# First layer's cosine: one read of PSUM, the argument in turns, and 2 pi applied to the stored sums

## The chip, the cores and the metric

The kernel runs on one core of one Trainium2 chip. The metric is the device time of one execution in microseconds (us); lower is better. Within the core, TensorE (PE in the profile) multiplies, VectorE (DVE), ScalarE (ACT) and GpSimd (POOL) work elementwise, and SyncE (SP) issues the transfers. They run at the same time and meet at semaphores. Each takes its own instructions in a fixed order.

## The reference

An attention with packed keys, then two layers of the same build, each a product, an elementwise function and a second product. The change lies in the elementwise function of the first layer, `h * cos(h)`.

```python
def _attn_ref(q, k, v, p):                     # (8, 8, 576, 64); p: (8, 8, 32, 64)
    p_packed = sm_attn(p, k, v)                # softmax attention of 32 queries per head
    return sm_attn(q, p_packed, p_packed)

def _moe_ref(x, w_in, w_out):                  # first layer: x (4608, 512), w_in (512, 2048)
    h = x @ w_in
    g = h * np.cos(h)
    return (g @ w_out).astype(np.float32)

def _moe2_ref(x, w_in, w_out):                 # second layer
    h = x @ w_in
    sp = np.where(h > 20.0, h, np.log1p(np.exp(np.minimum(h, 20.0))))
    return ((h * np.tanh(sp)) @ w_out).astype(np.float32)

x = attn_out.transpose(0, 2, 1, 3).reshape(B * S, H * D)
x = _moe_ref(x=x, **moe_kwargs)
return _moe2_ref(x=x, **moe2_kwargs)
```

All tensors are fp32 (weights come in as 64-bit numbers and are converted on the chip).

## The kernel before, in words

The program has two stages. Stage one holds the attention and the first layer, stage two the second layer. This text calls 40 to 845 us of the profiled execution stage one's main part: it is where the 256 units described next run.

The 4608 tokens are cut into 16 tiles of 288, and the 2048 columns of the hidden layer into 16 slices of 128. A *unit* is one slice of one tile, so `h` comes in 256 blocks of 128x288. For a unit, TensorE first computes `h` with six matmuls (`l1`): every fp32 operand is kept as a high part rounded to fp32r and a low rest, and `mm3` adds three products (lines L145, L146, L147; two such triples for the two halves of the inner dimension). The result lies in one buffer of a PSUM ring of four, named `ps`. The same ring serves the attention's matmuls, in the background.

Then comes the chain of elementwise work of the unit:

- `chain_first`: ACT reads `ps`, scales by 1/(2 pi), adds 0.25 and rounds to an integer `ki` (L802). DVE reads `ki` and `ps` and forms `r = ps - 2 pi * ki` (L804). DVE clamps `r` to the range that the sine takes (L805).
- `chain_cos`: ACT computes `sin(r + pi/2)` in place (L811). DVE multiplies it by `ps` (L812). This is the last read of `ps`, and frees the ring's buffer.
- `chain_split`: ACT rounds the product to the high part `gh[:, 0]` (L819; `G_ACT = (0, 1)` with `G_MOD = 2` puts every unit there), and POOL computes the low part `gh[:, 1]` (L822), which frees the buffer of `r` (four of them).

Three units behind, `l2` multiplies `gh` by the second weight `wo` with twelve matmuls into four PSUM accumulators `acc` (again L145 to L147). After 16 units, `evac` copies the four accumulators to SBUF, two on ACT (L843) and two on DVE (L845), and stores them to DRAM (`x2d`), where stage two picks them up.

Between the units' instructions stands background work for later tiles: loads, transposes, softmax and projections of the attention, conversions of weights (L436, L437, L441, L581 to L583), and splits of weights for stage two. The source says after how many units each piece is given out. The order on each engine, though, is made by the framework's scheduler, which runs the program against its own model of durations, with priorities written in the source (`HP_L1`, `HP_CHAIN`, and others). A changed duration or dependency can therefore move instructions anywhere in stage one.

DVE operations are told apart below by where their tensor inputs lie: L804 and L812 have one input in SBUF and one in PSUM; L441 has two in SBUF; L805 has one, in SBUF.

Of the kernel before, what the change touches and what calls it, by code (L numbers as in the profile page):

```python
# [8 lines left out]
F32 = mybir.dt.float32  # L9
F32R = mybir.dt.float32r  # L10
I32 = mybir.dt.int32
AF = mybir.ActivationFunctionType
ALU = mybir.AluOpType
# [5 lines left out]
TT = 288  # L19
# [3 lines left out]
NBT = NTOK // BT  # L23
LAG_A = 3
G_MOD = 2
G_ACT = (0, 1)
C_MOD = 2
C_POOL = ()
W_POS = ((57, 1.1), (55, 1.2), (52, 1.2))
K_LD = 3  # L30
Q_LD = 2
# [51 lines left out]
TWO_PI = 2.0 * math.pi  # L83
# [4 lines left out]
def build(tc, q, k, v, p, w1i, w1o, w2i, w2o, out):  # L88
    nc = tc.nc
    ctx = ExitStack()  # L90
    with ctx:
        wpool = ctx.enter_context(tc.tile_pool(name="wpool", bufs=1))
# [5 lines left out]
        def nm(s):  # L98
            cnt[0] += 1
            return f"{s}_{cnt[0]}"  # L100
# [17 lines left out]

        ident = wpool.tile([128, 128], F32, name="ident")
        make_identity(nc, ident)  # L120
        halfpi = wpool.tile([128, 1], F32, name="halfpi")
        nc.vector.memset(halfpi, math.pi / 2)
        quarter = wpool.tile([128, 1], F32, name="quarter")
        nc.vector.memset(quarter, 0.25)
        wpool.tile([128, 8], F32, name="gap_w")
# [6 lines left out]
        ap = apool_cm.__enter__()  # L132
# [575 lines left out]
        for j in range(16):  # L708
            ms[j], load, cs = w_load(j // 4, j % 4, True)
            n = W0_STEP[j]  # L710
# [7 lines left out]
        for ft in range(16):  # L718
            load, cs = wo1_unit(ft)
            n = ft + WO_OFF  # L720
# [9 lines left out]
        for j in range(16):  # L730
            ms[j], load, _ = w_load(j // 4, j % 4)
            n = W01[0] + int(W01[1] * j)
# [20 lines left out]
        for pair in range(3):  # L753
# [9 lines left out]
            for j in range(16):  # L763
                ms[j], load, _ = w_load(j // 4, j % 4)
                n = n0 + W_POS[pair][0] + int(W_POS[pair][1] * (j // 2 * 2 + 1))
# [5 lines left out]
        for t in range(1, NT):  # L771
            n = Q_N[t - 1]
# [25 lines left out]

        def chain_first(n):
            st = hst[n]  # L800
            ki = ap.tile([128, TT], I32, tag="ki", bufs=2, name=nm("ki"))
            nc.scalar.activation(ki, st["h"], AF.Identity, bias=quarter, scale=1.0 / TWO_PI)  # L802
            r = ap.tile([128, TT], F32, tag="r", bufs=4, name=nm("r"))
            nc.vector.scalar_tensor_tensor(r, ki, -TWO_PI, st["h"], ALU.mult, ALU.add)  # L804
            (nc.gpsimd if n % C_MOD in C_POOL else nc.vector).tensor_scalar(r, r, 1.570796, -4.712388, ALU.min, ALU.max)  # L805
            st["r"] = r

        def chain_cos(n):
            st = hst[n]
            g = st["r"]  # L810
            nc.scalar.activation(g, g, AF.Sin, bias=halfpi, scale=1.0)  # L811
            nc.vector.tensor_tensor(g, g, st["h"], ALU.mult)  # L812
            st["g"] = g

        def chain_split(n):
            st = hst[n]
            gh = ap.tile([128, 2, TT], F32R, tag="gh", bufs=GH_BUFS, name=nm("gh"))
            if n % G_MOD in G_ACT:
                nc.scalar.copy(gh[:, 0], st["g"])  # L819
# [17 lines left out]
        def evac(t):  # L837
            for dc in range(4):
                o = ap.tile([128, TT], F32, tag="xo", bufs=3, name=nm("xo"))
                x = acc[t][dc][:, :TT].rearrange("p (a s) -> p s a", s=32)  # L840
                y = o.rearrange("p (s a) -> p s a", s=32)
                if dc % 2 == 0:
                    nc.scalar.copy(y, x)  # L843
                else:
                    nc.vector.tensor_copy(y, x)  # L845
                nc.sync.dma_start(x2d[t][:, dc, :], o)

        X = {}
# [62 lines left out]
        for n in range(NA + LAG_A):  # L911
            if STOP and n >= STOP:
                apool_cm.__exit__(None, None, None)
                return
            if n < NA:
                with tc.high_priority(offset=HP_L1):
                    l1(n)
            run_bg(bg_pe, n)
            m = n - LAG_A
            if m >= 0:  # L920
                l2(m)
            with tc.high_priority(offset=HP_CHAIN):
                if 1 <= n <= NA:
                    chain_cos(n - 1)
                if n < NA:
                    chain_first(n)
                if 1 <= n <= NA:
                    chain_split(n - 1)
            run_ew(n)
            if m >= 0 and m % NF == NF - 1:  # L930
                evac(m // NF)
# [268 lines left out]
```

## Time and profile before

| | |
|---|---|
| median of 3 runs | 1555.14 us (1553.41 to 1558.32) |
| the profiled execution's own time | 1555.48 us |
| its span, first to last instruction | 1552.9 us |
| PE, PEld busy | 1475.9 us (95%), 1278.3 us (82%) |
| DVE, ACT, POOL busy | 1117.8 (72%), 883.9 (57%), 639.2 us (41%) |
| mean granted TensorE clock | 0.989 of full speed |

PE is the matmul side of TensorE, PEld its loading of weights, which overlaps the matmuls. A busy PE is not a PE at its peak: in full flow the matmuls of stage one start 0.13 us apart and each is shown as about 0.3 us long, so their spans overlap. What matters is the idle time before an instruction and the instruction that ended it (the *releaser*). A wait of PE means that matmuls had run out; a wait of PEld means that the next weights could not be loaded, which comes a little earlier.

### The profile page before, as it was taken

What the parts mean: (1) busy time and instruction counts of PE and PEld (TensorE: products, weight loads), DVE (VectorE), ACT (ScalarE), POOL (GpSimd) and SP (SyncE); (2) the same over time, 40 slices, a digit from 0 to 9 for tenths busy, and PEclk for the clock granted to TensorE, in tenths of its full rate; (3) what the DMA queues carried; (4) which work ended last, traced back from release to release, by engine and by line L of the source; (5) the groups of instructions that cost most, each with busy time, mean ns of one, the idle gap of its engine ahead of it and who ended that gap; (6) DMA issues with size and microseconds to landing.
All of it is one profiled execution on the core that took longest, in us unless ns stands there. A gap on an engine that the chain in (4) does not pass through costs nothing.

```text
span 1552.9 us, 28652 instructions
## 1 busy us (share of the span) xinstructions
PE 1475.9 (95%) x9728; PEld 1278.3 (82%) x9728; DVE 1117.8 (72%) x2082; ACT 883.9 (57%) x1838; POOL 639.2 (41%) x634
## 2 busy tenths in 40 slices
PE   3789999999999999999999999999999999999998
PEld 1567778788987898788999887888889898888997
DVE  4896666777776877678675878678668857766756
ACT  3675767666667677667665455344443534454443
POOL 0462333245643544627754666223522622352102
PEclk9899999999999999999999999999999999999999
DMA  9889676436648457533313767668868877877887
GB/s 293 283 214 226 170 184 161 123 101 176 186 122 225 139 152 195 163 107 104 104 49 98 259 217 241 193 196 242 266 212 235 298 223 219 244 205 221 241 257 202
DMA packets 247377, 300.75 MB, mean 194 GB/s; under 512 B 104384, under 2 KB 129472, under 8 KB 247232
## 3 DMA queue, kind: packets, MB, share of 16 engines
q1 hardware_dynamic: 246432, 298.73, 66.1%
q8 instruction: 77, 1.26, 0.3%
q14 instruction: 68, 0.56, 0.1%
q10 hardware_dynamic: 800, 0.20, 0.1%
HBM read 242.22 MB, written 56.62 MB: 192 GB/s over the span
## 4 chain that ended last, share of the span: by engine, by line
PE 50%; DVE 6%; ACT 3%; issue 2%; DMA 2%; POOL 1%; SPq 0%; DVEq 0%; ACTq 0%; POOLq 0%
PE acc L146 9%; PE acc L147 9%; PE acc L145 9%; PE ps L145 8%; PE ps L147 8%; PE ps L146 8%; DVE r L805 1%; ACT r L811 1%; DVE r L812 1%; DVE r L804 1%; DMA raw<-in_moe_w_in_dram 1%; DVE wab L897 1%; ACT wab L896 1%; PE ps L491 0%; DMA tst<-wt 0%
## 5 line engine op out<-in xcount | busy, mean ns | idle before, releaser
L822 POOL TENSOR_TENSOR gh<-r,gh 128x288 fp32r<-128x288 f32 x256 | 214.9, 847 | 334.3 <-ACT gh L819 231.7
L146 PE MATMUL acc<-gh,wo 128*128 128x288 f32 x1024 | 301.5, 301 | 2.2 <-POOL gh L822 1.7
L147 PE MATMUL acc<-gh,wo 128*128 128x288 f32 x1024 | 298.2, 298 | 0.0
L955 POOL TENSOR_TENSOR gh<-t,gh 128x512 fp32r<-128x512 f32 (+1 forms) x108 | 144.2, 1340 | 351.5 <-ACT gh L954 290.7
L145 PE MATMUL acc<-gh,wo 128*128 128x288 f32 x1024 | 273.7, 304 | 2.1 <-ACT gh L819 1.9
L145 PEld LDWEIGHTS acc<-gh,wo 128*128 128x128 f32 x1024 | 181.2, 190 | 34.6 <-issue 11.9
L146 PE MATMUL acc<-gh,T 128*128 128x512 f32 (+1 forms) x560 | 207.0, 371 | 2.2 <-DVE gh L955 1.7
L145 PE MATMUL ps<-wab,ws 128*128 128x512 f32 (+1 forms) x560 | 206.0, 369 | 1.8 <-ACT gh L954 0.8
L146 PEld LDWEIGHTS acc<-gh,wo 128*128 128x128 f32 x1024 | 194.1, 190 | 15.9 <-issue 9.5
L146 PE MATMUL ps<-wab,ws 128*128 128x512 f32 (+1 forms) x560 | 206.4, 369 | 0.0
L147 PE MATMUL ps<-wab,ws 128*128 128x512 f32 (+1 forms) x560 | 205.4, 369 | 0.0
L147 PE MATMUL acc<-gh,T 128*128 128x512 f32 (+1 forms) x560 | 205.1, 369 | 0.0
L147 PEld LDWEIGHTS acc<-gh,wo 128*128 128x128 f32 x1024 | 194.2, 190 | 5.8 <-issue 5.6
L955 DVE TENSOR_TENSOR gh<-wo,gh 128x512 fp32r<-128x512 f32 (+1 forms) x160 | 128.7, 810 | 81.7 <-ACT gh L954 81.3
L811 ACT ACTIVATE r<-r,halfpi 128x288 f32<-128x288 f32 x256 | 136.3, 535 | 83.9 <-DVE r L805 81.6
L145 PE MATMUL acc<-gh,T 128*128 128x512 f32 (+1 forms) x560 | 181.9, 369 | 0.6 <-DMA T<-tst 0.5
L145 PE MATMUL ps<-aT,wab 128*128 128x288 f32 x512 | 159.7, 312 | 22.7 <-DVE r L812 16.5
L812 DVE TENSOR_TENSOR r<-r,ps 128x288 f32<-128x288 f32 x256 | 114.5, 449 | 73.3 <-ACT r L811 72.5
L802 ACT ACTIVATE ki<-ps,quarter 128x288 int32<-128x288 f32 x256 | 125.1, 496 | 59.7 <-PE ps L147 49.6
L804 DVE SCALAR_TENSOR_TENSOR r<-ki,ps 128x288 f32<-128x288 int32 x256 | 113.8, 447 | 55.8 <-ACT ki L802 39.5
L146 PE MATMUL ps<-aT,wab 128*128 128x288 f32 x512 | 152.2, 297 | 0.0
L147 PE MATMUL ps<-aT,wab 128*128 128x288 f32 x512 | 151.5, 296 | 0.0
(169 smaller groups left out, 2956.1 us busy)
## 6 DMA issues: line engine op xcount, KB each, us to landing
T<-tst SPq DMA_DIRECT2D x280, 256.0 KB, 3.1
ws<-wst SPq DMA_DIRECT2D x224, 256.0 KB, 3.0
ld<-ws SPq DMA_DIRECT2D x80, 256.0 KB, 3.5
kr<-in_k_dram SPq DMA_DIRECT2D x64, 272.0 KB, 5.6
kr<-in_q_dram SPq DMA_DIRECT2D x60, 272.0 KB, 6.0
tst<-wt SPq DMA_DIRECT2D x56, 256.0 KB, 2.6
wst<-ws SPq DMA_DIRECT2D x56, 256.0 KB, 2.5
x2d<-xo SPq DMA_DIRECT2D x64, 144.0 KB, 1.8
```

What stands on the lines that cost most here:

```text
L145: nc.tensor.matmul(ps, l0, r0, start=first, stop=False, skip_group_check=more)
L146: nc.tensor.matmul(ps, l0, r1, start=False, stop=False, skip_group_check=more)
L147: nc.tensor.matmul(ps, l1, r0, start=False, stop=last, skip_group_check=more)
L802: nc.scalar.activation(ki, st["h"], AF.Identity, bias=quarter, scale=1.0 / TWO_PI)
L804: nc.vector.scalar_tensor_tensor(r, ki, -TWO_PI, st["h"], ALU.mult, ALU.add)
L805: (nc.gpsimd if n % C_MOD in C_POOL else nc.vector).tensor_scalar(r, r, 1.570796, -4.712388, ALU.min, ALU.max)
L811: nc.scalar.activation(g, g, AF.Sin, bias=halfpi, scale=1.0)
L812: nc.vector.tensor_tensor(g, g, st["h"], ALU.mult)
L822: nc.gpsimd.tensor_tensor(gh[:, 1], st["g"], gh[:, 0], ALU.subtract)
L896: nc.scalar.copy(x[:, a, 0, :n], src)
L897: (nc.gpsimd if k % 2 == 0 else nc.vector).tensor_tensor(x[:, a, 1, :n], src, x[:, a, 0, :n], ALU.subtract)
L955: eng.tensor_tensor(hl[:, 1, :n], src, hl[:, 0, :n], ALU.subtract)
```

## The change

`f = h / (2 pi)` is written once from PSUM to SBUF by ACT, with no added constant (first instruction). A second ACT instruction reads `f` from SBUF, adds 0.25 and rounds to the integer `ki`, which lies in the bytes of `u`. One DVE operation then forms `u = f + 0.25 - ki`, between -0.5 and 0.5, so that no clamp is needed. The sine takes `2 pi * u`, without an added tensor, and DVE multiplies it by `f` instead of by `ps`. Since `f` is `h / (2 pi)`, the sums of the second product come out divided by 2 pi, and `evac` multiplies them by 2 pi where it copied them before. `G_ACT = (0,)` gives the rounding of the high part to ACT in every even unit and to DVE in every odd one.

```diff
-G_ACT = (0, 1)
-C_MOD = 2
-C_POOL = ()
+G_ACT = (0,)
...
         def chain_first(n):
             st = hst[n]
-            ki = ap.tile([128, TT], I32, tag="ki", bufs=2, name=nm("ki"))
-            nc.scalar.activation(ki, st["h"], AF.Identity, bias=quarter, scale=1.0 / TWO_PI)
-            r = ap.tile([128, TT], F32, tag="r", bufs=4, name=nm("r"))
-            nc.vector.scalar_tensor_tensor(r, ki, -TWO_PI, st["h"], ALU.mult, ALU.add)
-            (nc.gpsimd if n % C_MOD in C_POOL else nc.vector).tensor_scalar(r, r, 1.570796, -4.712388, ALU.min, ALU.max)
-            st["r"] = r
+            f = st["f"] = ap.tile([128, TT], F32, tag="f", bufs=4, name=nm("f"))
+            nc.scalar.activation(f, st["h"], AF.Identity, scale=1.0 / TWO_PI)
+            u = st["u"] = ap.tile([128, TT], F32, tag="u", bufs=2, name=nm("u"))
+            ki = u.bitcast(I32)
+            nc.scalar.activation(ki, f, AF.Identity, bias=quarter)
+            nc.vector.scalar_tensor_tensor(u, f, 0.25, ki, ALU.add, ALU.subtract)

         def chain_cos(n):
             st = hst[n]
-            g = st["r"]
-            nc.scalar.activation(g, g, AF.Sin, bias=halfpi, scale=1.0)
-            nc.vector.tensor_tensor(g, g, st["h"], ALU.mult)
-            st["g"] = g
+            f, u = st["f"], st["u"]
+            nc.scalar.activation(u, u, AF.Sin, scale=6.283185)
+            nc.vector.tensor_tensor(f, f, u, ALU.mult)
+            st["g"] = f
...
                 if dc % 2 == 0:
-                    nc.scalar.copy(y, x)
+                    nc.scalar.mul(y, x, TWO_PI)
                 else:
-                    nc.vector.tensor_copy(y, x)
+                    nc.vector.tensor_scalar(y, x, TWO_PI, None, ALU.mult)
```

The changed kernel's lines stand three lower: `mm3` is L142 to L144. Its chain is L799 (`f`, ACT), L802 (`ki`, ACT), L803 (`u`, DVE), L808 (sine, ACT), L809 (product, DVE), L816 or L818 (high part, ACT or DVE), L819 (low part, POOL).

The order changes as well. On ACT, around units 158 to 160 (`ki_1434`, `r_1435`, `f_1434` and `u_1435` belong to unit 158), before:

```order
L802 ACTIVATE ki_1434_7462<-ps_1433_7441,quarter_86 128x288
L819 CAST gh_1436_7467<-r_1429_7431 128x288
L802 ACTIVATE ki_1438_7491<-ps_1437_7470,quarter_86 128x288
L811 ACTIVATE r_1435_7464<-r_1435_7464,halfpi_84 128x288
L802 ACTIVATE ki_1444_7525<-ps_1443_7504,quarter_86 128x288
L819 CAST gh_1440_7496<-r_1435_7464 128x288
```

and the same place on ACT in the changed kernel:

```order
L799 ACTIVATE f_1434_7461<-ps_1433_7440 128x288
L808 ACTIVATE u_1429_7430<-u_1429_7430 128x288
L802 ACTIVATE u_1435_7463<-f_1434_7461,quarter_85 128x288
L799 ACTIVATE f_1438_7490<-ps_1437_7469 128x288
L802 ACTIVATE u_1439_7492<-f_1438_7490,quarter_85 128x288
L808 ACTIVATE u_1435_7463<-u_1435_7463 128x288
```

The read of `ps` stands where it stood, one unit ahead of the sine; a second ACT instruction has come in behind it, and half of the casts are gone.

On DVE, units 158 to 160, before:

```order
L804 SCALAR_TENSOR_TENSOR r_1435_7464<-ki_1434_7462,ps_1433_7441 128x288
L805 TENSOR_SCALAR r_1435_7464<-r_1435_7464 128x288
L804 SCALAR_TENSOR_TENSOR r_1439_7493<-ki_1438_7491,ps_1437_7470 128x288
L812 TENSOR_TENSOR r_1435_7464<-r_1435_7464,ps_1433_7441 128x288
L805 TENSOR_SCALAR r_1439_7493<-r_1439_7493 128x288
L804 SCALAR_TENSOR_TENSOR r_1445_7527<-ki_1444_7525,ps_1443_7504 128x288
```

and in the changed kernel:

```order
L803 SCALAR_TENSOR_TENSOR u_1435_7463<-f_1434_7461,u_1435_7463 128x288
L803 SCALAR_TENSOR_TENSOR u_1439_7492<-f_1438_7490,u_1439_7492 128x288
L809 TENSOR_TENSOR f_1434_7461<-f_1434_7461,u_1435_7463 128x288
L809 TENSOR_TENSOR f_1438_7490<-f_1438_7490,u_1439_7492 128x288
L803 SCALAR_TENSOR_TENSOR u_1445_7526<-f_1444_7524,u_1445_7526 128x288
L818 CAST gh_1436_7466<-f_1428_7428 128x288
```

The clamps are gone, a cast of every second unit has come in, and neither remaining operation reads `ps`.

On PE, at the first matmul of unit 162 (`ps_1455`), with what the instruction waits for, before:

```order
L145 MATMUL acc3_1351_6995<-gh_1424_7400,wo_213_979 128x288
L146 MATMUL acc3_1351_6995<-gh_1424_7400,wo_213_979 128x288
L147 MATMUL acc3_1351_6995<-gh_1424_7400,wo_213_979 128x288
L145 MATMUL ps_1455_7579<-aT_1415_7340,wab_1108_5738 128x288 [waits DVE_49]
L146 MATMUL ps_1455_7579<-aT_1415_7340,wab_1108_5738 128x288
```

and in the changed kernel:

```order
L142 MATMUL acc2_1350_6993<-gh_1414_7336,wo_194_891 128x288
L143 MATMUL acc2_1350_6993<-gh_1414_7336,wo_194_891 128x288
L142 MATMUL ps_1455_7578<-aT_1415_7339,wab_1108_5737 128x288 [waits Activation_49]
L143 MATMUL ps_1455_7578<-aT_1415_7339,wab_1108_5737 128x288
L144 MATMUL ps_1455_7578<-aT_1415_7339,wab_1108_5737 128x288
```

The matmul that takes a ring buffer waits for ACT where it waited for DVE, and it has moved ahead of some of `l2`'s matmuls. Over the 256 units the first matmul waits for DVE in 208 cases before and in 38 now, for ACT in 31 before and in 180 now. On average 3.8 later units have their `l1` in front of a unit's `l2` before, and 4.8 now. ACT's table loads in the chain and the softmax go from 47 to 51.

## Rows read from the trace of the kernel before

**Rows 1.** Busy us by stretch: length, PE, PEld, DVE, ACT, POOL; clock, DMA, GB/s.

```profile
40.00:100.00 60.00, 46.58 (x289) 34.61 (x290) 56.15 (x100) 43.63 (x84) 31.77 (x27) 0.82 0.83 254
100.00:845.00 745.00, 718.28 (x5939) 627.92 (x5938) 528.13 (x1189) 505.58 (x1102) 346.17 (x392) 0.99 0.55 147
845.00:1553.00 708.00, 698.50 (x3355) 610.02 (x3353) 513.84 (x747) 321.96 (x626) 258.18 (x207) 1.00 0.76 232
...
553.00:845.00 292.00, 283.68 (x2208) 259.61 (x2205) 206.08 (x444) 196.40 (x433) 158.11 (x178) 1.00 0.38 112
```

**Rows 2.** Waits of PE, whole span: total us, times, longest.

```profile
PE ps L145 <- DVE r L812: 16.5, 18, 6.2
...
PE acc L145 <- ACT gh L819: 1.9, 5, 0.6
PE ps L351 <- DVE r L812: 1.8, 1, 1.8
...
PE ps L218 <- DVE r L812: 1.0, 2, 0.6
```

**Rows 3.** Waits of PEld, 40 to 845 us.

```profile
PEld ps L145 <- DVE r L812: 25.4, 27, 7.1
...
PEld ps L254 <- DVE r L812: 1.3, 1, 1.3
```

**Rows 4.** Groups by line: busy us, mean ns of one; idle before, releasers.

```profile
L822 POOL TENSOR_TENSOR gh<-r,gh 128x288 fp32r<-128x288 f32 x256 | 214.9, 847 | 334.3 <-ACT gh L819 231.7 <-issue 50.4 <-PE ps L147 9.4
...
L811 ACT ACTIVATE r<-r,halfpi 128x288 f32<-128x288 f32 x256 | 136.3, 535 | 83.9 <-DVE r L805 81.6 <-DVE r L812 0.9
L802 ACT ACTIVATE ki<-ps,quarter 128x288 int32<-128x288 f32 x256 | 125.1, 496 | 59.7 <-PE ps L147 49.6 <-DVE r L804 9.3
L805 DVE TENSOR_SCALAR r<-r 128x288 f32<-128x288 f32 x256 | 123.7, 487 | 4.9
L812 DVE TENSOR_TENSOR r<-r,ps 128x288 f32<-128x288 f32 x256 | 114.5, 449 | 73.3 <-ACT r L811 72.5
L804 DVE SCALAR_TENSOR_TENSOR r<-ki,ps 128x288 f32<-128x288 int32 x256 | 113.8, 447 | 55.8 <-ACT ki L802 39.5 <-POOL gh L822 14.4 <-POOL wt L596 0.5
L819 ACT CAST gh<-r 128x288 fp32r<-128x288 f32 x256 | 108.4, 428 | 47.5 <-DVE r L812 27.5 <-PE acc L147 15.0 <-DVE kt L156 2.0
...
L811 ACT ACT_TABLE_LOAD x24 | 30.8, 1283 | 0.4
...
L843 ACT COPY xo<-acc 128x288 f32<-128x288 f32 x32 | 12.2, 394 | 7.9 <-PE acc L147 7.9
```

**Rows 5.** Single DVE lines: duration ns min/median/max, first and last start, form.

```profile
L804 DVE SCALAR_TENSOR_TENSOR r<-ki,ps x256: 386/448/456, 50.7 to 832.5; 128x288 f32<-128x288 int32 x128
...
L805 DVE TENSOR_SCALAR r<-r x256: 253/311/1379, 51.5 to 833.0; 128x288 f32<-128x288 f32 x128
...
L441 DVE SCALAR_TENSOR_TENSOR tmp<-tmp,cvt x32: 645/692/1802, 42.6 to 690.0; 128x512 int32<-128x512 int32 x32
...
L544 DVE TENSOR_TENSOR ld<-ld,ld x8: 420/958/1293, 737.8 to 913.2; 128x256 f32<-128x256 f32 x8
```

**Rows 6.** Groups of 845 to 1553 us, shapes apart.

```profile
L955 DVE TENSOR_TENSOR gh<-wo,gh 128x512 fp32r<-128x512 f32 x96 | 89.0, 929 | 52.4 <-ACT gh L954 52.2
...
L1012 DVE TENSOR_TENSOR wo<-ps,u 128x512 f32<-128x512 f32 x72 | 48.6, 682 | 29.1 <-PE ps L147 28.7
L955 DVE TENSOR_TENSOR gh<-wo,gh 128x384 fp32r<-128x384 f32 x64 | 39.7, 632 | 29.3 <-ACT gh L954 29.1
...
L1012 DVE TENSOR_TENSOR wo<-ps,u 128x384 f32<-128x384 f32 x48 | 26.1, 549 | 16.6 <-PE ps L147 16.6
```

**Rows 7.** Chain of waits, 553 to 845 us: shares of that stretch.

```profile
by line: PE acc L145 9.8%; PE acc L146 9.7%; PE acc L147 9.5%; issue 7.9%; DVE r L805 5.4%; PE ps L145 4.8%; PE ps L147 4.5%; PE ps L146 4.4%; ACT r L811 4.1%; DVE r L812 3.9%; DVE r L804 3.7%; DMA raw<-in_moe_w_in_dram 3.5%; PE ps L491 2.1
```

**Rows 8.** The same chain, two pieces: start us, us, what.

```profile
578.12 0.47 DVE r L804
...
580.03 0.38 DVE r L804
```

More of the change, by code (lines that the diff above doesn't have):

```diff
@@ L120, in build @@
         make_identity(nc, ident)
-        halfpi = wpool.tile([128, 1], F32, name="halfpi")
-        nc.vector.memset(halfpi, math.pi / 2)
+        wpool.tile([128, 1], F32, name="gap_h")
         quarter = wpool.tile([128, 1], F32, name="quarter")
```

## The prediction

> **What bounds the kernel now.** I read busy time by stretch first, then the waits of TensorE, then the groups of the chain's lines, and last the chain of waits. PE is busy nearly all the time from 100 us on [rows 1], so the first guess is that only PE's own work or its waits can move the time. By stretch three parts differ. From 40 to 100 us PE is busy 46.6 of 60 us and DVE 56.2: DVE and the loads set the pace there. From 100 to 845 us PE is idle 745 - 718 = 27 us. From 845 us on, in the second layer, the change touches no instruction. So all that can be won lies ahead of 845 us, and it is in PE's waits. The largest by name is the wait of `l1`'s first matmul for DVE's product L812 [rows 2], 16.5 us in 18 waits: the ring of four PSUM buffers is full, and a buffer comes free only when the last instruction of the first half of the chain has read it. Background matmuls wait for the same line; the five groups together, of which the first and the last are shown, make 21.8 us in 23 waits [rows 2]. On the side of the weight loads the five groups make 34.9 us in 39 waits [rows 3], since loads run ahead of the matmuls. PE's waits for the finished product are small: 1.9 us for the high part [rows 2].
>
> How near the elementwise engines are to being late is in the chain of waits. Between 553 and 845 us, DVE's three chain lines hold 5.4 + 3.9 + 3.7 = 13.0% and the sine 4.1% of the stretch [rows 7]: 38 us and 12 us. In its bursts the chain goes round between DVE and ACT, one unit in 580.03 - 578.12 = 1.91 us at best [rows 8], because L804, L805, the sine and L812 of a unit follow one another with little between them.
>
> **Part one: the ring's buffer is free after ACT's first read.** Before, the buffer was held from `l1` through L802, L804, L805, L811 and L812. Now it is held through the read into `f` alone, which stands in ACT's order where L802 stood. By the means the release comes earlier by 447 + 487 + 535 + 449 = 1918 ns [rows 4], without the gaps between engines. The longest of PE's 23 waits is 6.2 us and the next 1.8 us [rows 2]. So all but the longest are covered by 1.92 us; the longest leaves 6.2 - 1.9 = 4.3 us. That gives back 21.8 - 4.3 = 17.5 us. By the load side, the longest is 7.1 us and leaves 5.2, which gives 34.9 - 5.2 = 29.7 us. In full flow the matmuls of stage one start one weight load apart, so the load side is the truer measure of lost time, while part of it is still covered by matmuls under way. I take 22 us, nearer to PE's row, and keep 0 and 30 as ends: 0 if another wait ends last at each of these places.
>
> **Part two: ACT has more to do.** `f` is a read of PSUM without an added tensor: between the copy L843 (394 ns) and L802 (496 ns) [rows 4]; I take 405, near the copy. The second instruction is SBUF to SBUF with an added tensor, as the sine is now: 535. The sine loses its added tensor: between 428 (L819) and 535, I take 440, near L819. The cast stays for half of the units: 428 / 2 = 214. Sum 1594 ns against 496 + 535 + 428 = 1459 before: +135 ns, times 256 = +35 us. Four more table loads at 1283 ns [rows 4] add 5 us: +40 us. With both choices at their upper ends a unit takes 1780 ns (+82 us in place of +35), at their lower 1571 (+29 us). What of it reaches the end: the sine holds 12 us of the chain while ACT is busy 196 us in that stretch [rows 1, 7], 6%. So 40 x 0.06 = +2.4 us.
>
> **Part three: DVE loses the clamp and gets half the casts, and its two other operations have both inputs in SBUF.** The clamp goes: -487 ns. Half the casts, one SBUF input of the same size, as the clamp was: 487 / 2 = +244. For L803 and L809 no row of before has this shape. Read alone they should take what L804 and L812 take: in the second layer 128x512 from PSUM takes 682 ns [rows 6], and for the same size the median of L441, two SBUF inputs, is 692 [rows 5]. But the form with a PSUM input is never long (L804 at most 456 ns), while L441 reaches 1802, and L805 has a median of 311, a mean of 487 and a maximum of 1379 [rows 4, 5]. What makes them long is read from the other rows: where POOL works, DVE's two-SBUF forms are longer in the mean than the PSUM form of the same shape, by 632 - 549 = 83 ns (128x384) and by 929 - 682 = 247 ns (128x512) [rows 6]; in stage one, L805's mean is 176 above its median. The L544 sums, while POOL splits weights, have a median 538 above their minimum [rows 5]. I take +175 per operation, as L805's, which runs at the same places; ends 0 and 538.
>
> The Trainium skill says the same as a rule, and it speaks against this change: SBUF — State Buffer, section "Who interferes with whom", has a DVE instruction with two SBUF inputs contend with a GpSimd instruction that reads SBUF, and one with a single SBUF input (outside the two-port modes) not. The trace agrees, in that L804 with its PSUM input stays within 456 ns and L441 does not stay near its median. The rule has the second to issue stand still until the first is done; an estimate by it: POOL is busy 346 of 745 us [rows 1], and whoever meets one of its operations waits for half of it, 847 / 2 ns for L822 [rows 4], which gives 0.46 x 424 = 197 ns in place of 175, and a sum of 1543 in place of 1541.
>
> So DVE's chain goes from 447 + 487 + 449 = 1383 to 622 + 624 + 244 = 1490 ns: +107, times 256 = +27 us. With +0 and a cast at L805's median it is 1052 ns (-85 us), with +538 it is 2216 ns (+213 us). Of DVE's 206 busy us in 553 to 845, 38 lie on the chain of waits [rows 1, 7], 18%: 27 x 0.18 = +4.9 us, ends -15 and +38. From 40 to 100 us, where DVE is full, the share is higher, but few of the 256 units run there.
>
> **Costs of nothing.** `evac`'s multiplications take the place of copies that read the same PSUM data on the same engines, 64 in all; a change of 20 ns each would be 1.3 us of busy time, beside PE's matmuls. The loop that bounded the bursts gets shorter: `f` and `ki` of the next unit can run ahead, and what must follow is L803, sine, L809, 622 + 440 + 624 = 1.69 us where it was 1.91 us or more; I count nothing for it, since the shares of parts two and three were taken from stretches that hold the longer round.
>
> **The sum.** -22 + 2.4 + 4.9 = -14.7 us on the profiled execution's own 1555.5 us: 1540.8, which I round to 1541. That execution stands 0.3 us above the median of the runs shown, so nothing has to be shifted.
>
> **The rivals.**
>
> *The wait only changes its name.* `f` has four buffers, and the fifth waits until POOL's low part of four units earlier is done. Before, that wait fell on DVE's L804: 14.4 us [rows 4]. Now it falls on ACT, ahead of the read that frees the ring, and what is queued behind it on ACT is the sine of the previous unit, the casts and the softmax of the background. For it: POOL's operation is the end of the chain, and units now run 4.8 ahead, not 3.8. Against it: POOL is busy only 346 of 745 us [rows 1]. If PE gets all 14.4 us back, the time is 1541 + 14 = 1555, no change.
>
> *Slower: DVE's two operations stand behind POOL.* The mechanism is that of part three at a higher price, with its place in the 256 units where POOL's L822 and DVE's L803 and L809 of neighbouring units meet. It decides once DVE's growth times 0.18 eats 22 - 2.4 = 19.6 us: 109 us, 425 ns per unit, which is (425 - 107) / 2 + 175 = 334 ns above the undisturbed time of each operation, or means near 780 ns. At L544's 538 DVE grows by 213 us: 1555.5 - 22 + 2.4 + 38 = 1574. For it: the 128x512 rows have 247 although POOL is busy only 258 of 708 us there, against 346 of 745 in stage one [rows 1, 6]. Against it: an operation of 288 columns is shorter than one of 512, and 128x384 shows only 83.
>
> *More is won.* The load side measures the loss, the shorter round of the chain pays for ACT and DVE, and all 29.7 us come back: 1555.5 - 29.7 = 1526.
>
> **How the numbers follow.** About 5 us (0.3%) is what a measurement of this kernel can tell from no change. The forecast, 1541 with its own range of 1531 to 1550, has a chance of 0.49; more is won 0.13; the wait changes its name 0.17; slower 0.21. Faster is the first two, 0.62. For 8 in 10 the range reaches from just below the largest gain, 1524, to 1562, where the slower case begins to weigh: it leaves out over half of that case, some 0.12, and about 0.06 below.
>
> **What would show it.** Right: waits of PE's `ps` matmuls for L809 are gone, and those for L799 make under 5 us; idle PE between 100 and 845 us falls from 27 to about 10 us. L803 and L809 have means near 620 ns, with maxima above 1 us, and L799 near 405, L802 near 535, L808 near 440. Everything from the first matmul of the second layer on is as long as before. Wrong: PE waits for the cast (L816, L818) or POOL's L819 in place of the ring, DVE's means near 780 ns, or ACT waiting for POOL in front of L799 for more than 15 us.

## The result: 1572.5 us, slower, and the profile after

The changed kernel takes 1572.51 us (median of 5 runs, 1571.29 to 1574.4) against 1554.44 us of the kernel before beside it: 18 us more, a ratio of 1.0115 with a 95% interval of 1.0099 to 1.0132. The forecast was 1541, and its range ended at 1562: the sign was wrong, and the time lies outside. The profiled execution takes 1574.4 us, with a span of 1572.5.

First the busy time by stretch, columns as in [rows 1]:

```profile
40.00:100.00 60.00, 45.56 (x288) 33.11 (x289) 55.29 (x92) 43.53 (x89) 36.59 (x28) 0.89 0.82 257
100.00:845.00 745.00, 700.08 (x5787) 613.29 (x5786) 537.48 (x1051) 531.10 (x1206) 363.65 (x384) 0.98 0.54 145
864.00:1572.00 708.00, 700.04 (x3366) 611.73 (x3364) 513.82 (x748) 323.25 (x627) 257.50 (x207) 1.00 0.76 232
553.00:845.00 292.00, 275.19 (x2120) 252.48 (x2120) 215.62 (x389) 208.57 (x481) 166.89 (x175) 0.98 0.40 117
```

The second layer begins at 864.6 us, where it began at 843.6, and then takes 708 us where it took 709: all of the loss is in stage one. There PE stands idle for 745 - 700 = 45 us where it was 27 [rows 1]. DVE, ACT and POOL are all busier, by 9, 26 and 17 us. The granted clock of the whole span is 0.986 against 0.989, 0.3% less, which is 5 of the 18 us at most. The waits of TensorE tell what ends its idle times, with columns as in [rows 2]: the changed kernel in all of stage one, then ahead of 100 us alone; and the kernel before ahead of 100 us and, last, from 100 us on:

```profile
PE ps L142 <- ACT f L799: 9.4, 9, 3.6
...
PE acc L143 <- POOL gh L819: 6.7, 8, 1.5
PE acc L142 <- ACT gh L816: 6.1, 5, 2.0
...
PE ps L142 <- DVE wab L508: 5.4, 3, 2.4
```

```profile
PE ps L142 <- ACT wab L507: 5.3, 1, 5.3
```

```profile
PE ps L145 <- DVE r L812: 6.7, 2, 6.2
...
PE ps L351 <- DVE r L812: 1.8, 1, 1.8
```

```profile
PE ps L145 <- DVE r L812: 9.8, 16, 1.0
```

The waits for the product [rows 2] are gone, as the change intends. In their place stand waits for ACT's read L799, for the high and low parts, and for casts of the background (L508, L507). And the split shows what whole-span totals hide: 6.7 + 1.8 = 8.5 of the 21.8 us, the longest wait among them, lay ahead of 100 us, where DVE and the loads set the pace. There one wait of 5.3 us for ACT's cast L507 has come in, and PE is busy 58.1 us of these 100 where it was 59.2: nothing was won there.

The groups by line answer to [rows 4], the single lines to [rows 5]:

```profile
L819 POOL TENSOR_TENSOR gh<-f,gh 128x288 fp32r<-128x288 f32 x256 | 231.1, 906 | 325.7 <-ACT gh L816 148.0 <-DVE gh L818 121.1 <-issue 19.3
...
L803 DVE SCALAR_TENSOR_TENSOR u<-f,u 128x288 f32<-128x288 f32 x256 | 159.4, 628 | 48.1 <-ACT u L802 46.5
...
L809 DVE TENSOR_TENSOR f<-f,u 128x288 f32<-128x288 f32 x256 | 151.8, 599 | 67.4 <-ACT u L808 64.0 <-POOL raw L599 2.2 <-ACT gh L816 0.6
L802 ACT ACTIVATE u<-f,quarter 128x288 int32<-128x288 f32 x256 | 135.6, 534 | 9.9 <-DVE f L809 5.4
L808 ACT ACTIVATE u<-u 128x288 f32<-128x288 f32 x256 | 112.3, 442 | 85.8 <-DVE u L803 84.6
L799 ACT ACTIVATE f<-ps 128x288 f32<-128x288 f32 x256 | 102.9, 404 | 39.7 <-POOL gh L819 21.8 <-PE ps L144 16.6
...
L818 DVE CAST gh<-f 128x288 fp32r<-128x288 f32 x128 | 58.6, 458 | 7.7 <-PE acc L144 4.5
L816 ACT CAST gh<-f 128x288 fp32r<-128x288 f32 x128 | 54.6, 426 | 37.6 <-DVE f L809 26.9 <-PE acc L144 9.1 <-PE ps L144 1.2
```

```profile
L803 DVE SCALAR_TENSOR_TENSOR u<-f,u x256: 387/459/1683, 52.8 to 855.0; 128x288 f32<-128x288 f32 x128
```

```profile
L809 DVE TENSOR_TENSOR f<-f,u x256: 410/459/1681, 56.1 to 856.4; 128x288 f32<-128x288 f32 x128
```

Every duration is close to its forecast: L803 628 ns (622), L809 599 (624), L799 404 (405), L802 534 (535), L808 442 (440), the casts 458 on DVE (487) and 426 on ACT (428). DVE's two operations have a median of 459 ns, 10 above the PSUM form of before, and single ones reach 1.68 us, where L804 never passed 456 ns. POOL's L819 has become longer too, 906 ns against 847. So the prices were right, and what they do to the end was not.

What makes the long ones long can be read from the trace one by one. POOL, then DVE, around 222 us:

```profile
221.69 1.64 POOL L391 TENSOR_TENSOR aT<-tmp,aT 128x576 fp32r<-128x576 f32 x1
223.29 1.02 POOL L819 TENSOR_TENSOR gh<-f,gh 128x288 fp32r<-128x288 f32 x1
```

```profile
222.06 1.59 DVE L803 SCALAR_TENSOR_TENSOR u<-f,u 128x288 f32<-128x288 f32 x1
223.57 1.05 DVE L809 TENSOR_TENSOR f<-f,u 128x288 f32<-128x288 f32 x1
```

L803 starts while POOL's L391 runs and ends 0.32 us after it. L819 starts before that end and is done 0.66 us after it, and L809 in turn ends 0.31 us after L819. All 170 instances of L803 and L809 above 0.5 us are like this: each overlaps an operation of POOL and ends 310 to 319 ns after one ends. They hold 82 us beyond the median, nearly all of the growth. So DVE's operation stands still until POOL's is done, and POOL's can stand still behind DVE's.

The chain of waits in the same stretch of stage one as [rows 7], prolonged to its end, shows how little such shares tell of it:

```profile
by line: PE acc L143 10.6%; PE acc L142 10.6%; PE acc L144 10.4%; issue 6.4%; PE ps L142 5.4%; DMA raw<-in_moe_w_in_dram 5.3%; PE ps L144 4.6%; PE ps L143 4.6%; DVE u L803 3.9%; POOL gh L819 3.4%; POOL wt L593 2.6%; DVE f L809 2.4%; ACT f L
```

DVE's chain lines hold 3.9 + 2.4 = 6.3% of it, half of the 13.0% of before, and the kernel is slower.

### The profile page after: what moved, and what is told of

It reads as the page before. It is cut to its first block, busy times and chain, and to the rows that moved or that the text cites. A ratio compares the mean times of both kernels' runs of the same rounds, so it can differ in the third digit from the quotient of the medians.

```text
span 1572.5 us, 28451 instructions
## 1 busy us (share of the span) xinstructions
PE 1477.2 (94%) x9728; PEld 1282.9 (82%) x9728; DVE 1134.6 (72%) x1953; ACT 920.1 (59%) x1970; POOL 668.0 (42%) x634
## 4 chain that ended last, share of the span: by engine, by line
PE 61%; DVE 12%; ACT 9%; DMA 9%; issue 4%; POOL 4%; SPq 1%; DVEq 0%; ACTq 0%; POOLq 0%
PE acc L142 10%; PE acc L143 10%; PE acc L144 10%; PE ps L142 9%; PE ps L144 9%; PE ps L143 9%; DVE u L803 2%; DVE f L809 2%; DMA kr<-in_k_dram 2%; DMA raw<-in_moe_w_out_dram 2%; DMA raw<-in_moe_w_in_dram 2%; PE ps L488 1%; ACT f L799 1%; DVE kt L153 1%; ACT u L808 1%
## 5 line engine op out<-in xcount | busy, mean ns | idle before, releaser
L819 POOL TENSOR_TENSOR gh<-f,gh 128x288 fp32r<-128x288 f32 x256 | 231.1, 906 | 325.7 <-ACT gh L816 148.0
L143 PE MATMUL acc<-gh,wo 128*128 128x288 f32 x1024 | 305.8, 302 | 7.1 <-POOL gh L819 6.7
L142 PE MATMUL acc<-gh,wo 128*128 128x288 f32 x1024 | 291.3, 304 | 14.0 <-ACT gh L816 6.1
L144 PE MATMUL acc<-gh,wo 128*128 128x288 f32 x1024 | 301.1, 298 | 0.0
L142 PEld LDWEIGHTS acc<-gh,wo 128*128 128x128 f32 x1024 | 188.3, 191 | 36.9 <-issue 15.3
L143 PEld LDWEIGHTS acc<-gh,wo 128*128 128x128 f32 x1024 | 195.7, 191 | 15.4 <-POOL gh L819 10.0
L142 PE MATMUL ps<-wab,ws 128*128 128x512 f32 (+1 forms) x560 | 205.9, 368 | 1.0 <-DVE wo L1009 0.4
L144 PE MATMUL ps<-wab,ws 128*128 128x512 f32 (+1 forms) x560 | 205.3, 369 | 0.0
L144 PE MATMUL acc<-gh,T 128*128 128x512 f32 (+1 forms) x560 | 205.1, 369 | 0.0
L809 DVE TENSOR_TENSOR f<-f,u 128x288 f32<-128x288 f32 x256 | 151.8, 599 | 67.4 <-ACT u L808 64.0
L144 PEld LDWEIGHTS acc<-gh,wo 128*128 128x128 f32 x1024 | 195.2, 191 | 2.7 <-issue 2.5
L803 DVE SCALAR_TENSOR_TENSOR u<-f,u 128x288 f32<-128x288 f32 x256 | 159.4, 628 | 48.1 <-ACT u L802 46.5
L142 PE MATMUL ps<-aT,wab 128*128 128x288 f32 x512 | 163.3, 319 | 21.6 <-ACT f L799 9.4
L142 PE MATMUL acc<-gh,T 128*128 128x512 f32 (+1 forms) x560 | 182.0, 369 | 0.1
L808 ACT ACTIVATE u<-u 128x288 f32<-128x288 f32 x256 | 112.3, 442 | 85.8 <-DVE u L803 84.6
L143 PE MATMUL ps<-aT,wab 128*128 128x288 f32 x512 | 153.3, 300 | 0.4 <-POOL aT L391 0.4
L144 PE MATMUL ps<-aT,wab 128*128 128x288 f32 x512 | 152.8, 299 | 0.0
L142 PEld LDWEIGHTS ps<-aT,wab 128*128 128x128 f32 x512 | 98.3, 192 | 57.8 <-ACT f L799 14.9
```

Source lines behind the costliest of these rows:

```text
L142: nc.tensor.matmul(ps, l0, r0, start=first, stop=False, skip_group_check=more)
L143: nc.tensor.matmul(ps, l0, r1, start=False, stop=False, skip_group_check=more)
L144: nc.tensor.matmul(ps, l1, r0, start=False, stop=last, skip_group_check=more)
L803: nc.vector.scalar_tensor_tensor(u, f, 0.25, ki, ALU.add, ALU.subtract)
L808: nc.scalar.activation(u, u, AF.Sin, scale=6.283185)
L809: nc.vector.tensor_tensor(f, f, u, ALU.mult)
```

## The experiments

Ten kernels ran. Ratios are to the kernel before, run beside them on the same chip, with their 95% intervals.

| kernel | median us | ratio |
|---|---|---|
| changed kernel | 1572.51 | 1.0115 (1.0099 to 1.0132) |
| a_poolset | 1549.38 | 0.9957 (0.9935 to 0.9979) |
| b_poolset | 1543.20 | 0.9924 (0.9900 to 0.9948) |
| a_sine32 | 1564.33 | 1.0062 (1.0046 to 1.0077) |
| a_castact | 1567.64 | 1.0087 (1.0062 to 1.0112) |
| a_psumprod | 1561.94 | 1.0047 (1.0029 to 1.0066) |
| a_psumboth | 1552.41 | 0.9985 (0.9970 to 0.9999) |
| a_psumboth_poolset | 1551.15 | 0.9959 (0.9940 to 0.9978) |
| b_noclamp | 1544.26 | 0.9928 (0.9903 to 0.9954) |
| b_noclamp_half | 1544.27 | 0.9932 (0.9913 to 0.9951) |
| b_noclamp_r5 | 1539.65 | 0.9891 (0.9873 to 0.9909) |

Names that begin with a_ are made from the changed kernel, with b_ from the one before. Three theories stood at the start: A, DVE's operations with two SBUF inputs collide with POOL's; B, ACT's longer turn is the loss; C, the newly placed order is.

**Take the reads of POOL's low part away, in both kernels (a_poolset, b_poolset).** POOL's other operations stay. In both, in the finished order of instructions:

```diff
-            nc.gpsimd.tensor_tensor(gh[:, 1], st["g"], gh[:, 0], ALU.subtract)
+            nc.gpsimd.memset(gh[:, 1], 0)     # in the same place of POOL's order
```

> The changed kernel with every engine's order and waits kept, but POOL's low part of each unit (L819) writes a constant zero over the 128x288 instead of a difference: it reads no SBUF, and the low part of the product is left out. Theory A (DVE's two operations and its cast collide with POOL's reads of SBUF, and what stands behind them on DVE comes late): L803 and L809 fall from means of 628 and 599 to about 460 to 520 (POOL's background work still reads), and the time falls by 15 us or more, to 1550 to 1558. Theory B (ACT's longer turn): L803 and L809 fall as well, but the time stays above 1565. Theory C (the order the scheduler made is the cause): the time falls by as much as in the kernel before under the same edit, so that the two stay about 18 us apart.

> The same edit on the kernel before, its orders kept: POOL's low part (L822) is a constant zero and reads no SBUF. Only the clamp L805 and background operations collided with it. Theory A: a small gain, 0 to 8 us (1546 to 1555), since L804 and L812 never collided, and the distance to the changed kernel under this edit is under 6 us. Theory C: the distance stays near 18 us.

The groups of a_poolset, then of b_poolset:

```profile
L803 DVE SCALAR_TENSOR_TENSOR u<-f,u 128x288 f32<-128x288 f32 x256 | 136.1, 537 | 48.5 <-ACT u L802 46.9
...
L809 DVE TENSOR_TENSOR f<-f,u 128x288 f32<-128x288 f32 x256 | 128.7, 508 | 71.9 <-ACT u L808 64.0 <-POOL gh L819 4.3 <-POOL raw L599 2.2
...
L819 POOL MEMSET gh<- 128x288 f32 x256 | 87.1, 342 | 412.1 <-ACT gh L816 204.9 <-DVE gh L818 169.8 <-DVE sm L228 8.4
```

```profile
L812 DVE TENSOR_TENSOR r<-r,ps 128x288 f32<-128x288 f32 x256 | 114.5, 450 | 74.1 <-ACT r L811 73.4
...
L805 DVE TENSOR_SCALAR r<-r 128x288 f32<-128x288 f32 x256 | 109.1, 430 | 4.9
...
L822 POOL MEMSET gh<- 128x288 f32 x256 | 87.7, 346 | 423.4 <-ACT gh L819 307.5 <-issue 67.1 <-DVE r L805 10.1
```

By the ratios the changed kernel gains 0.0158 x 1555 = 24.6 us, the one before 11.8. Of the changed kernel's surplus of 18 us about 5 are left. L803 and L809 lose 91 ns each while L812 keeps its 450, so A carries most of it and C, whose order was held, does not. A's figures were missed all the same: L803 stays at 537 ns (460 to 520 expected), a_poolset ends 1 us below its range, and b_poolset gains 11.8 us where 0 to 8 were expected. This pair alone can't say how much is collision and how much POOL's own shorter operation.

**Shorten ACT (a_sine32), or move all casts to ACT (a_castact).**

```diff
-            nc.scalar.activation(u, u, AF.Sin, scale=6.283185)
+            nc.scalar.activation(u[:, :32], u[:, :32], AF.Sin, scale=6.283185)   # a_sine32, order held
```

```diff
-G_ACT = (0,)
+G_ACT = (0, 1)      # a_castact
```

> The changed kernel with all orders and waits kept, but ACT's sine (L808) works on 32 of 288 columns; the sine of the others is left out. That takes about 210 ns of each unit from ACT, 54 us in all, more than the 40 us that the change added there. Theory B: the time falls to 1545 to 1558. Theory A: it falls by less than 7 us, as DVE's operations keep their length. Theory C: likewise little.

> The changed kernel with G_ACT = (0, 1): every cast of the high part on ACT, as before the change; the scheduler orders it anew. DVE loses 128 casts (434 ns each, 55 us), ACT gets 128 casts (428 ns each, 55 us). Theory A: faster than the changed kernel by 3 to 10 us, to 1562 to 1569. Theory B: slower, 1575 to 1590.

```profile
L803 DVE SCALAR_TENSOR_TENSOR u<-f,u 128x288 f32<-128x288 f32 x256 | 169.8, 669 | 48.3 <-ACT u L802 46.6
...
L808 ACT ACTIVATE u<-u 128x32 f32<-128x32 f32 x256 | 57.9, 228 | 103.2 <-DVE u L803 101.5
```

The sine is 442 - 228 = 214 ns shorter, 55 us of ACT's time, and 8 us come back by the medians: ACT's time has a price, but too small a one for B, whose range (1545 to 1558) is missed; A, which allowed less than 7 us, is missed by 1 us, within the noise. DVE's operations stay long. With all casts on ACT, which B expected at 1575 to 1590, the time is 1567.64, below the changed kernel by 5 us with intervals that overlap. B alone is refuted by both.

**Give DVE its PSUM inputs back, one at a time (a_psumprod, a_psumboth).** a_psumprod:

```diff
-            nc.vector.tensor_tensor(f, f, u, ALU.mult)
+            nc.vector.tensor_tensor(f, u, st["h"], ALU.mult)      # and evac copies as before
```

a_psumboth has this, and

```diff
-            nc.vector.scalar_tensor_tensor(u, f, 0.25, ki, ALU.add, ALU.subtract)
+            nc.vector.scalar_tensor_tensor(u, st["h"], 1.0 / TWO_PI, ki, ALU.mult, ALU.subtract)
-            nc.scalar.activation(u, u, AF.Sin, scale=6.283185)
+            nc.scalar.activation(u, u, AF.Sin, bias=halfpi, scale=6.28315)
```

> The changed kernel with the product alone reading PSUM (ps times the cosine, and so no 2 pi at the evacuation); the ring's buffer is held through the product again, and L803 keeps its two SBUF inputs. Theory A: the product comes down from 599 to about 450 ns, L803 stays near 630; half of the collisions go, some 6 us, and PE's waits for the ring come back at up to 10 us: 1564 to 1578. Theory R (the early release is worth the 22 us that the prediction gave it, and more is lost elsewhere): 1580 to 1595.

> The changed kernel with both of DVE's operations reading the argument from PSUM again: u is ps times 1/2 pi minus the integer, and the product is ps times the cosine; ACT's two operations f and ki stay as they are, the sine has its added tensor again (about +100 ns per unit on ACT), and the ring's buffer is held through the product again. Theory A (DVE's operations with two SBUF inputs collide with POOL's, about +190 and +160 ns each): both come down to about 450 ns, as L804 and L812 of before, with no maximum above 0.6 us, and 1545 to 1560 us although the ring's waits of PE come back. Theory B (ACT's longer turn is the loss): ACT has more to do than in the changed kernel, 1575 to 1590. Theory C (the loss is in the order in which the instructions were placed): no prediction of the direction, but DVE's shorter operations move little, 1565 to 1575.

The single lines of DVE, a_psumprod's two first, then a_psumboth's two, and the groups of a_psumboth:

```profile
L803 DVE SCALAR_TENSOR_TENSOR u<-f,u x256: 390/459/1655, 53.7 to 844.0; 128x288 f32<-128x288 f32 x128
```

```profile
L809 DVE TENSOR_TENSOR f<-u,ps x256: 407/453/457, 57.1 to 845.4; 128x288 f32<-128x288 f32 x128
```

```profile
L810 DVE TENSOR_TENSOR f<-u,ps x256: 406/454/458, 55.3 to 831.3; 128x288 f32<-128x288 f32 x128
```

```profile
L804 DVE SCALAR_TENSOR_TENSOR u<-ps,u x256: 389/453/460, 51.8 to 829.7; 128x288 f32<-128x288 f32 x128
```

```profile
L820 POOL TENSOR_TENSOR gh<-f,gh 128x288 fp32r<-128x288 f32 x256 | 212.5, 835 | 317.9 <-ACT gh L817 143.5 <-DVE gh L819 128.6 <-issue 16.2
...
L809 ACT ACTIVATE u<-u,halfpi 128x288 f32<-128x288 f32 x256 | 134.9, 532 | 42.4 <-DVE u L804 39.3
L810 DVE TENSOR_TENSOR f<-u,ps 128x288 f32<-128x288 f32 x256 | 114.5, 450 | 72.9 <-ACT u L809 66.8 <-POOL gh L820 2.9 <-POOL wt L594 0.6
L804 DVE SCALAR_TENSOR_TENSOR u<-ps,u 128x288 f32<-128x288 f32 x256 | 114.4, 450 | 65.8 <-ACT u L803 64.7
L800 ACT ACTIVATE f<-ps 128x288 f32<-128x288 f32 x256 | 102.2, 401 | 62.2 <-PE ps L145 50.7 <-POOL gh L820 10.3
```

An operation that gets its PSUM input back never passes 460 ns, though in a_psumboth 316 of the 512 overlap an operation of POOL; the one that keeps two SBUF inputs still reaches 1.66 us, beside the same POOL. Each step gives time back, 10.6 us for the product and 9.6 us for L803, although the ring's buffer is held through the product again and the sine has become 90 ns longer. Together 20 us. The poolset kernels, the next one among them, give a like size by another way: taking the low part's reads out is worth 24.6 us in the changed kernel and (0.9985 - 0.9959) x 1555 = 4 us where DVE reads PSUM; the 21 us between them are what two SBUF inputs cost beside POOL's low part alone. a_psumboth lies in A's range; B expected 1575 to 1590 for it, since ACT has more to do there than in the changed kernel (936 us busy in all against 920). a_psumprod ends 2 us below A's range, which had counted up to 10 us for the ring's waits; the next run takes that up. POOL's operation, too, is back from 906 to 835 ns.

The Trainium skill (SBUF — State Buffer, section "Who interferes with whom") says which forms these are: a DVE instruction with two SBUF inputs contends with GpSimd's reads, one with a single SBUF input outside the two-port modes doesn't. These rows agree with both halves.

**Hold the ring, with POOL's low part out of the way (a_psumboth_poolset).** The edit of a_psumboth and the one of a_poolset together.

> The changed kernel with both of DVE's operations reading PSUM, and POOL's low part replaced by a zero of the same place and size in POOL's order; the low part itself is left out. Against the changed kernel with that replacement alone (1549.4 us, its two-input operations at 537 and 508 ns), it holds the ring's buffer through the product. Theory S (the early release is worth little, since other waits end at the same places): 1540 to 1550, not above that kernel by more than 3 us, PE's waits for the product up to 17 us. Theory R (it is worth the 22 us of the prediction, and was hidden by the collisions): 1562 to 1575.

TensorE's waits in a_poolset, which frees the buffer early, then in a_psumboth_poolset, which holds it; then both kernels between 100 and 845 us, in that order; last, a_poolset's product:

```profile
PE acc L142 <- ACT gh L816: 6.3, 6, 1.5
...
PE ps L142 <- ACT wab L507: 5.1, 1, 5.1
PE ps L142 <- ACT f L799: 4.9, 5, 3.3
...
PE ps L142 <- DVE wab L508: 4.4, 3, 2.1
```

```profile
PE ps L143 <- DVE f L810: 17.1, 12, 7.0
```

```profile
100.00:845.00 745.00, 716.92 (x5976) 633.93 (x5976) 501.30 (x1080) 542.75 (x1239) 236.70 (x398) 1.00 0.55 151
```

```profile
100.00:845.00 745.00, 720.12 (x5936) 630.44 (x5935) 462.09 (x1067) 556.47 (x1227) 224.55 (x393) 0.99 0.54 147
```

```profile
L809 DVE TENSOR_TENSOR f<-f,u x256: 410/459/1670, 56.1 to 823.0; 128x288 f32<-128x288 f32 x128
```

The 17.1 us of waits for the product are there in one kernel and absent in the other, and the ratios are 0.9959 and 0.9957: no difference to within some 4 us, as S has it (the median is 1 us above S's range), and far from R's 1562. PE's idle time between 100 and 845 us is 28 us in the kernel that frees the ring early and 25 in the one that holds it, with waits for the casts, for L799 and for the background in the first. These two profiled executions are not alike, though (1543.0 us, the fastest of its kernel, and 1552.0), so the ratios decide.

The pair does not isolate the ring. a_poolset still collides with POOL's other operations: its two DVE operations take (537 - 450) + (508 - 450) = 145 ns per unit more than the others', 37 us in all. What such time costs can be estimated from the step from a_psumboth to a_psumprod, which leaves the ring as it is: L803 grows from 450 to 665 ns there, 55 us in all, and the time by 9.6 us, 17%. At that price the 37 us cost 6 us, and the early release would have to be worth as much for the two kernels to be equal. The sine without its added tensor, 90 ns shorter, and another order differ as well. So the release is worth 0 to some 10 us here, by this estimate and the noise. The step from a_psumprod to the changed kernel speaks against 22 too: DVE's two operations grow by (628 + 599) - (665 + 448) = 114 ns per unit, 29 us, and the time by 10.6; with 22 us won by the release, these 29 us would have to cost 33.

**The clamp alone (b_noclamp, b_noclamp_half).** The kernel before without the clamp:

```diff
-            nc.vector.scalar_tensor_tensor(r, ki, -TWO_PI, st["h"], ALU.mult, ALU.add)
-            (nc.gpsimd if n % C_MOD in C_POOL else nc.vector).tensor_scalar(r, r, 1.570796, -4.712388, ALU.min, ALU.max)
+            nc.vector.scalar_tensor_tensor(r, st["h"], 1.0 / TWO_PI, ki, ALU.mult, ALU.subtract)
-            nc.scalar.activation(g, g, AF.Sin, bias=halfpi, scale=1.0)
+            nc.scalar.activation(g, g, AF.Sin, bias=halfpi, scale=6.28315)
-G_ACT = (0, 1)
+G_ACT = (0,)        # in b_noclamp_half only
```

> The kernel before without the clamp: DVE makes ps times 1/2 pi minus the integer in one operation with one PSUM and one SBUF input, the sine takes 2 pi, just below it, as its scale and half pi as its added tensor, the product reads ps. ACT's work is that of before, DVE's is 487 ns per unit less, the ring is held for 0.49 us less. Theory A: DVE's two operations at about 450 ns each, none collides with POOL; by the forecast's share of 18 percent, 125 us less of DVE's time is 22 us, so 1530 to 1545. Theory D (DVE's time is not what the end hangs on, POOL and PE's own order are): 1549 to 1556.

> As the kernel before without the clamp, with the cast of every second unit on DVE, as in the changed kernel: per unit ACT has 214 ns less and DVE some 220 ns more, and the casts on DVE, with one SBUF input, are the only new thing there. Theory A (the cast has a mean of 434 ns on DVE because some of its instances meet POOL): about what the kernel before without the clamp gives, within 6 us either way, 1528 to 1548. Theory E (casts on DVE are what cost the changed kernel its 18 us): 10 us or more above that kernel.

b_noclamp by groups and in the long stretch:

```profile
L811 DVE TENSOR_TENSOR r<-r,ps 128x288 f32<-128x288 f32 x256 | 114.6, 450 | 86.1 <-ACT r L810 85.6
L804 DVE SCALAR_TENSOR_TENSOR r<-ps,ki 128x288 f32<-128x288 f32 x256 | 113.7, 452 | 79.6 <-ACT ki L802 42.6 <-POOL gh L821 33.2 <-POOL aT L394 1.2
```

```profile
100.00:845.00 745.00, 724.25 (x6007) 637.91 (x6006) 441.90 (x967) 518.73 (x1126) 347.03 (x402) 1.00 0.56 153
```

Of the change it has only the clamp's going: 11 us below the kernel before, inside A's range and clear of D's. PE is idle 21 us. Half of the casts on DVE change nothing measurable (0.9928, 0.9932), so the casts are not what costs (E is refuted). a_psumboth differs from b_noclamp_half in ACT's first part: ACT writes `f` (401 ns) and makes `ki` from it (535 ns, where the read from PSUM took 496), 113 us of ACT's time by the means, and (0.9985 - 0.9932) x 1555 = 8 us. The wait for a free buffer, too, falls on ACT there, no longer on DVE.

**One more buffer (b_noclamp_r5).**

```diff
-            r = ap.tile([128, TT], F32, tag="r", bufs=4, name=nm("r"))
+            r = ap.tile([128, TT], F32, tag="r", bufs=5, name=nm("r"))
```

> The kernel before without the clamp, with five buffers of r in place of four. In the version with four DVE's first operation waits 33.2 us in 36 waits for POOL's low part of four units earlier. Theory S (that wait delays the chain, and through it PE's waits for the high part and the product, 19.6 us in 8 waits): 1538 to 1543. Theory D (it is in the chain's slack): 1543 to 1547, as with four.

DVE's waits, b_noclamp first, then b_noclamp_r5:

```profile
DVE r L804 <- POOL gh L821: 33.2, 36, 2.9
```

```profile
DVE r L804 <- POOL gh L821: 23.3, 24, 3.6
```

It is the fastest kernel here, 17 us below the one before (ratio 0.9891), and in the range of S. The wait falls by a third only. The intervals of the two versions touch, so that the fifth buffer helps is likely, not shown.

## Why the prediction was wrong, step by step

From before to after by way of the kernels that ran, each step a difference of ratios times 1555 us, good to 4 or 5 us:

| step | us | forecast |
|---|---|---|
| the clamp goes (b_noclamp) | -11.2 | in part three |
| half of the casts to DVE (b_noclamp_half) | +0.6 | in part three |
| ACT writes `f` and makes `ki` from it (a_psumboth) | +8.2 | in part two |
| L803 reads SBUF alone, sine without its added tensor (a_psumprod) | +9.6 | parts three, two |
| the product reads SBUF alone, the ring is free early, 2 pi at `x` (changed kernel) | +10.6 | parts three, one |

They add up to the 18 us by construction; each kernel was put in order anew, so small steps hold a share of the order too. The collisions, though, have a like size with the order held (a_poolset).

**Part one, -22 us: failed, and the largest part of the miss.** The step that failed is from waits to time: the prediction took the waits for L812 as time that comes back. They went, as forecast, but others stood at these places, for L799, for casts of the background and for L816, L818 and L819 (the last three were the prediction's own sign of being wrong); idle PE between 100 and 845 us rose from 27 to 45 us, and the release is worth 0 to some 10 us in the one pair that differs by it and lets a bound be worked out. The prediction named this as its end of 0, "if another wait ends last at each of these places". I had also counted 8.5 us from ahead of 100 us, a stretch of which the prediction itself said that DVE and the loads set its pace. And I took the larger load-side total as support, though both sides only count who was last.

**Part two, +2.4 us: too small.** I added up ACT's gains and losses to +135 ns and took 6%. By runs, what ACT gained in front costs 8 us, 7% of 113 us, and moving half of the casts to DVE gives nothing back that can be measured (+0.6 us). So the share was about right, and the netting was not.

**Part three, +4.9 us: prices right, share wrong.** That the +175 ns, borrowed from L805, a form with one SBUF input, fits to 3 and 26 ns is in part luck. The +107 ns of net growth holds two things of unlike worth. The clamp took 487 ns x 256 = 125 us and its going is worth 11 us, 9%. The collisions put (628 - 450) + (599 - 450) = 327 ns x 256 = 84 us on DVE and cost 20 us, 24%, or more by what the early release gives back, which is in the same steps. A likely reason is in the rows: a collision makes POOL late as well (906 against 835 ns), and POOL's part ends the chain. That the long single operations, up to 1.68 us, also meet the bursts at the worst places is argued, not shown. At 18% for both, the net was +4.9; by runs it is -11.2 + 0.6 + 20.2 = +9.6, the release included.

So with the release put at 0, 0 + 8.2 + 9.6 = 17.8 us stand where the prediction had -22 + 2.4 + 4.9 = -14.7; if it gives up to 10 us, the collisions cost as much more.

**The rivals.** "Slower" named the right mechanism and nearly the right time (1574), for a wrong reason: it wanted means near 780 ns and started from part one's -22 us. With so little won by the ring, 600 to 630 ns were enough. "The wait only changes its name" holds as well: ACT waits for POOL ahead of L799, with the sign that the prediction set at 15 us, and it waits less for PE (49.6 us ahead of L802 before [rows 4]), as it would if it ran behind:

```profile
ACT f L799 <- POOL gh L819: 21.8, 45, 1.2
...
ACT f L799 <- PE ps L144: 16.6, 18, 2.3
```

**Costs of nothing** held: the second layer is as long as before, and the multiplications at the evacuation (402 and 449 ns) take what the copies took (394 and 453). What stays open is how the 10.6 us of the last step divide between collision and ring: no run frees the ring early without a second SBUF input on DVE.

## What to carry to other kernels

A wait of the busiest engine that is removed is worth at most the distance to the next thing that is late at the same place; before counting it, look in short stretches at what else ends there, and count nothing where the prediction itself says that something else sets the pace. Don't net gains and losses of one engine and multiply by one share: price each by whether it also delays its neighbour. And before an operand is moved from PSUM to SBUF to free a buffer, check whether its reader then has two SBUF inputs beside a busy GpSimd; here dropping the operation (the clamp) and leaving the operands in PSUM was better than the whole change by 28 us.

## What was not expected of the hardware

With POOL busy about half of the time, DVE's 128x288 operations with two SBUF inputs keep a median of 459 ns and have means of 599 to 669; the mean comes from single ones of up to 1.68 us, and in the changed kernel each one above 0.5 us ends about 315 ns after an operation of POOL ends. The product's SBUF form, with POOL's 256 reads replaced by writes of zeros, still reaches 1.67 us, with a mean of 508, beside POOL's other operations. And POOL pays too: its own low part takes 835 ns beside PSUM readers and 906 beside SBUF readers.
